# Folding two experts' partial sums in memory, and a queue of split work for VectorE and ScalarE

## The chip, the cores and the metric

The kernel runs on one core of a Trainium2 chip. The metric is device time in microseconds (us) of one execution; less is better. All matrix products run on TensorE (PE) with fp32 data. A product in enough precision takes three passes: each operand is split into a high part (`hi`, rounded to fp32r) and the rest (`lo = x - hi`), and hi·hi, lo·hi and hi·lo are added up in PSUM. ScalarE (ACT) writes the high parts, VectorE (DVE) the rests. GpSimd (POOL) and SyncE (SP) mostly issue DMAs.

## The reference

A gated linear recurrence over 768 steps (per batch and head) makes `x`, and a dense mixture of four experts is applied to it. Only the second part is touched here:

```python
# N, D, E, F = 3072, 384, 4, 1024
p = domain_probs / (domain_probs.sum(-1, keepdims=True) + 1e-09)
out = np.zeros((N, D), dtype=np.float32)
for e in range(E):
    h = np.maximum(x @ w1[e], 0.0)
    out += p[:, e:e + 1] * (h @ w2[e])
```

## The kernel before

**First phase** (to about 597 us). Twelve groups of 256 tokens. While DVE, ACT and DMAs make the recurrence of the next group, PE also applies experts 0 and 1 to the group before (`moe1`). At the end of each expert, `done` scales the two PSUM tiles by the token's probability on ACT and stores them with a DMA from POOL's queue into DRAM: `acc_d[g][e]`, one DRAM tile for each expert.

**Second phase** (597 us to the end). Experts 2 and 3, each over four blocks of 768 tokens, which makes eight rounds `R` = 0 to 7 (0 to 3 are expert 2). A block is two halves of 384 tokens (`u` = 0, 1). In a round there are four calls of `unit`, `j` = 0 to 3, each for two of the eight columns of hidden features. `unit` is a fast scheme of matrix multiplication: 11 products in place of 12, each 3 matmuls of 128x384, made from sums and differences of the weights (`prep_w`) and of the inputs (`prep_x`). It uses four PSUM banks `a`, `b`, `c`, `d` and these steps, in which a PSUM bank is added onto again after DVE has read what stood there:

- `a` and `m1` (ACT copies `a`), `b`, then `mp = b + m1` on DVE; `c`; `fill(0)`
- `b` goes on (product `s3`), so it needs `mp` to have been read; then `mq = b + m1`, `mq += c`, `d`, `mq += d` on DVE, ACT makes the hidden high part `hhb` of `mq`, DVE the rest `hlb`
- `a` goes on and gives another `hhb`, `hlb`; `fill(1)`
- `b` goes on (product `a22`), so it needs the first `mq` to have been read; then `m1 = b + m1` and its `hhb`, `hlb`
- `c` goes on; `mp = c + mp` and its `hhb`, `hlb`; `fill(2)`, `fill(3)`

The banks are taken in turn, so the next unit's `c` writes where this unit's `c` stood, and needs its `mp`. `fill(k)` puts in 9 matmuls of the second layer (`pob`) of an earlier hidden column. Round 0 has two fills in a unit, the later rounds four. Beside the `hlb` work, DVE adds each half's second layer into the accumulated output (`acc`, three instructions for each half, at `fill(1)` of the even units from round 1 on).

Between these steps `bg(k)` places work for later rounds, four places in a unit:

- `acc_add` (round 0 to 3, units 1 and 3): the two DRAM tiles of experts 0 and 1 were loaded by `acc_load` into `acc` and `prv`, and three DVE additions of 128x384 fold them.
- `prep_x` of the next round: 3 sums at the end of unit 2, and in unit 3 the splits of nine 128x384 inputs (`xh` on ACT, `xl` on DVE) with one more difference.
- `prep_w` of expert 3, four weight pairs, each begun in rounds 1, 2, 3 and 4: splits of weights (`whi`, `wlo`, `shi`, `slo`) and four short sums, spread one part at a time over the places 0 and 3 of units 0 to 2.

All DVE, ACT, SP and PE instructions of this phase are held to the order in which the code writes them (`pin`, `pe`), each engine runs its own list in order, and engines wait for one another by semaphores. The loads of inputs, weights and accumulated outputs are all in SP's list.

Of the kernel before, what the change touches and what calls it, by code (L numbers as in the profile page):

```python
# [16 lines left out]
HD = H * D  # L17
# [50 lines left out]
def fast_path(ctx, tc, qkP, aP, vP, probsP, w, out, flag):  # L68
# [34 lines left out]
    acc_d = [[dram.tile([P, CG, HD], F32, name=f"acc_d{g}_{e}") for e in range(E1)] for g in range(NG)]  # L103
# [125 lines left out]
    with ExitStack() as c1:  # L229
# [417 lines left out]
        def moe1(g, xh, xl, between=None, prev=None):  # L647
            def done(e, po):
                acc = moe.tile([P, CG, HD], F32, tag="acc", name=f"acc{g}_{e}")
                for t in range(CG):  # L650
                    nc.scalar.activation(acc[:, t, :], po[t], AF.Copy, scale=pr[:, g * CG + t, e:e + 1])
                nc.gpsimd.dma_start(acc_d[g][e], acc)
            mo.block(g, xh, xl, 0, NF1, done, between, prev)
# [172 lines left out]
    with ExitStack() as c2:  # L826
# [38 lines left out]
        def prep_w(e, j):  # L865
            i = e * FE + 2 * j
            sts = []
            for u in range(2):
                st = stage2(i + u)
                pin(nc.sync.dma_start(st, w[i + u]))  # L870
                sts.append(st)
            yield 0
            (st0, st1), hs = sts, []
            for u in range(2):
                hi2 = wpool.tile([P, 2 * HD], F32R, tag="whi", name=f"whi{i + u}")
                lo2 = wpool.tile([P, 2 * HD], F32R, tag="wlo", name=f"wlo{i + u}")
                split(hi2[:, u * P:], lo2[:, u * P:], sts[u][:, u * P:])
                hs.append((hi2, lo2))
                yield 2
            (h0, l0), (h1, l1) = hs  # L880
            if j % 2 == 0:
                shared[e] = (wpool.tile([P, 2 * HD], F32R, tag="whi", name=f"shi{i}"),
                             wpool.tile([P, 2 * HD], F32R, tag="wlo", name=f"slo{i}"))
            hs, ls = (x[:, (j % 2) * HD:(j % 2 + 1) * HD] for x in shared[e])
            s = stage2(i)[:, :4 * P]
            tt(s[:, cut(0)], st1[:, cut(0)], st1[:, cut(1)], ALU.add)
            tt(s[:, cut(1)], s[:, cut(0)], st0[:, cut(0)], ALU.subtract)
            tt(s[:, cut(2)], st0[:, cut(0)], st1[:, cut(0)], ALU.subtract)
            tt(s[:, cut(3)], st0[:, cut(1)], s[:, cut(1)], ALU.subtract)
            yield 2  # L890
            split(hs, ls, s[:, :3 * P])
            split(h1[:, cut(0)], l1[:, cut(0)], s[:, cut(3)])
# [8 lines left out]
            yield 2  # L901
# [17 lines left out]
        def prep_x(R, xs, X):  # L919
            (b11, b21, b31), (b12, b22, b32) = ([x[:, k, :] for k in range(NJ)] for x in xs)  # L920

            def put(nm, src):
                X[nm] = split(fin.tile([P, TB2], F32R, tag="xoh", name=f"xh{R}_{nm}", bufs=9),
                              fin.tile([P, TB2], F32R, tag="xol", name=f"xl{R}_{nm}", bufs=9), src)

            t2, t3 = (fin.tile([P, TB2], F32, tag=nm, name=f"{nm}_{R}", bufs=1) for nm in ("t2", "t3"))
            tt(t3, b22, b12, ALU.subtract)
            tt(b12, b12, b11, ALU.subtract)
            tt(t2, b22, b12, ALU.subtract)
            yield  # L930
            put("b11", b11)
            put("t2", t2)
            put("t1", b12)
            yield
            put("t3", t3)
            put("b21", b21)
            tt(b21, b21, t2, ALU.subtract)
            yield
            put("t4", b21)
            put("b32", b32)  # L940
            put("b31", b31)
            put("b22", b22)
            yield
# [26 lines left out]
        def unit(R, j, X, fill, bg):  # L970
# [12 lines left out]
            bg(0)  # L983
# [31 lines left out]
        def acc_load(R, u):  # L1015
            e, b = E1 + R // NB2, 2 * (R % NB2) + u
            got = []
            for t in range(C2):
                c = b * C2 + t
                acc = fin.tile([P, HD], F32, tag="acc2", name=f"acc2_{R}_{u}_{t}", bufs=6)  # L1020
                prv = None
                if e == E1:
                    pin(nc.sync.dma_start(acc, acc_d[c // CG][0][:, c % CG, :]))
                    prv = moe.tile([P, HD], F32, tag=("hh", "hl")[t % 2], name=f"prv{R}_{u}_{t}")
                    pin(nc.sync.dma_start(prv, acc_d[c // CG][1][:, c % CG, :]))
                else:
                    pin(nc.sync.dma_start(acc, acc2_d[c]))
                got.append((acc, prv))
            accs[R, u] = got
# [8 lines left out]
        def l2(R, u, f):  # L1038
# [13 lines left out]
            for t in range(C2):  # L1052
                c, acc = b * C2 + t, accs[R, u][t][0]
# [9 lines left out]
        for _ in prep_w(E1, 0):  # L1063
            pass
        for _ in prep_x(0, xs, X):
            pass
        for j in range(1, NP):
            for _ in prep_w(E1, j):
                pass
        held["on"] = True  # L1070
        jobs, new, nxt = [], {}, None
        late = {(1, 0): 0, (2, 0): 1, (NB2 - 1, 3): 2, (NB2, 0): 3}
        for R in range(NR2):
            for j in range(NP):
                if (R, j) in late:
                    jobs.append(prep_w(E1 + 1, late[R, j]))
                    next(jobs[-1])
                if j == 0:
                    acc_load(R, 0)
                    if R + 1 < NR2:  # L1080
                        nxt = prep_x(R + 1, load_x2(R + 1), new)
                if j == 2:
                    acc_load(R, 1)
# [8 lines left out]
                def bg(k, R=R, j=j):  # L1092
# [8 lines left out]
                unit(R, j, X, fill, bg)  # L1101
            if R + 1 < NR2:
                X = dict(new)
# [194 lines left out]
```

## Time and profile before

| What | us |
|---|---|
| median of 3 runs | 1005.82 (1005.23 to 1006.34) |
| the profiled execution | 1006.48 |
| its span in the profile | 1004.8 |
| busy: PE / weight loads / DVE / ACT / POOL | 966.6 / 939.5 / 744.7 / 409.9 / 48.4 |

The profile is of one execution. An engine's rows are groups or single instructions with their start, length and the idle time in front of them, with the engine and instruction that ended it. Buffer numbers are left out of names: `phb_3b` is bank `b` of unit 3 in any round. PE's instructions overlap: one of 128x384 is shown with about 0.33 us, but the next one starts 0.17 us after it.

### The profile page before, as it was taken

The numbers are of one execution on the slowest core, as the hardware profiler recorded it, in microseconds if no ns is written. First come the engines' busy times: TensorE is split into PE (matmuls) and PEld (weight loads), VectorE is DVE, ScalarE is ACT, GpSimd is POOL, SyncE is SP. The second block draws the span as 40 slices with busy tenths as digits, with TensorE's granted clock in tenths as the row PEclk, the third lists the DMA queues.
The fourth block names the chain that finished last, engine by engine and source line by source line (L and its number), as shares of the span: only waits on it lengthen the run. The fifth ranks groups of instructions, "written<-read, shape, count | busy, mean of one in ns | idle before, by whom it ended". The sixth has DMA issues, their size and how long they took to land.

```text
span 1004.8 us, 17383 instructions
## 1 busy us (share of the span) xinstructions
PE 966.6 (96%) x6810; PEld 939.5 (94%) x6810; DVE 744.7 (74%) x1610; ACT 409.9 (41%) x792; POOL 48.4 (5%) x90
## 2 busy tenths in 40 slices
PE   5899999999999999999999999899999899999997
PEld 2899998999999999999999999899999899999997
DVE  7789989798987989798942567867676777666651
ACT  7755525456364453636422443323222333222310
POOL 6030000000000000000000000000000000000000
PEclk9899999999999999999999999999999999999999
DMA  9585277474674836547171444132313242221111
GB/s 314 159 172 142 64 190 148 129 205 111 166 189 116 224 107 162 155 122 207 56 173 29 130 141 142 55 127 91 127 63 119 90 131 67 79 91 52 48 49 50
DMA packets 105131, 125.38 MB, mean 125 GB/s; under 512 B 7312, under 2 KB 91328, under 8 KB 105040
## 3 DMA queue, kind: packets, MB, share of 16 engines
q1 hardware_dynamic: 98928, 103.55, 37.5%
q0 software_dynamic: 6112, 20.63, 6.6%
q8 instruction: 55, 0.90, 0.4%
q14 instruction: 36, 0.29, 0.1%
HBM read 83.53 MB, written 40.62 MB: 124 GB/s over the span
## 4 chain that ended last, share of the span: by engine, by line


## 5 line engine op out<-in xcount | busy, mean ns | idle before, releaser
L198 PE MATMUL po<-whi,hh 128*128 128x384 f32 x384 | 129.6, 338 | 1.1 <-ACT hh L188 1.1
L198 PE MATMUL po<-wlo,hh 128*128 128x384 f32 x384 | 128.9, 336 | 0.0
L844 PE MATMUL pob<-whi,hlb 128*128 128x384 f32 x384 | 128.3, 334 | 0.0
L844 PE MATMUL pob<-whi,hhb 128*128 128x384 f32 x384 | 128.3, 334 | 0.0
L844 PE MATMUL pob<-wlo,hhb 128*128 128x384 f32 x384 | 128.3, 334 | 0.0
L198 PE MATMUL po<-whi,hl 128*128 128x384 f32 x384 | 124.1, 338 | 0.9 <-DVE hl L189 0.8
L188 ACT ACTIVATE hh<-ph 128x512 fp32r<-128x512 f32 x96 | 57.1, 595 | 145.0 <-PE ph L178 142.4
L178 PE MATMUL ph<-xha,whi 128*128 128x256 f32 x576 | 103.9, 286 | 1.2 <-ACT xha L165 1.2
L178 PE MATMUL ph<-xla,whi 128*128 128x256 f32 x576 | 100.9, 284 | 0.4 <-DVE xla L167 0.4
L178 PE MATMUL ph<-xha,wlo 128*128 128x256 f32 x576 | 101.3, 283 | 0.0
L189 DVE SCALAR_TENSOR_TENSOR hl<-ph,hh 128x512 fp32r<-128x512 f32 x96 | 66.0, 688 | 43.9 <-ACT hh L188 43.3
L178 PEld LDWEIGHTS ph<-xha,whi 128*128 128x128 f32 x576 | 85.9, 190 | 2.5 <-ACT xha L165 1.5
L178 PEld LDWEIGHTS ph<-xla,whi 128*128 128x128 f32 x576 | 82.5, 191 | 0.6 <-DVE xla L167 0.6
L178 PEld LDWEIGHTS ph<-xha,wlo 128*128 128x128 f32 x576 | 82.8, 190 | 0.2 <-issue 0.2
L198 PEld LDWEIGHTS po<-whi,hh 128*128 128x128 f32 x384 | 72.4, 189 | 1.5 <-ACT hh L188 1.3
L847 ACT ACTIVATE hhb<-mq 128x384 fp32r<-128x384 f32 x32 | 16.8, 526 | 138.9 <-DVE mq L850 138.9
L198 PEld LDWEIGHTS po<-whi,hl 128*128 128x128 f32 x384 | 70.9, 188 | 2.0 <-DVE hl L189 1.9
L198 PEld LDWEIGHTS po<-wlo,hh 128*128 128x128 f32 x384 | 72.5, 189 | 0.0
L844 PEld LDWEIGHTS pob<-whi,hlb 128*128 128x128 f32 x384 | 72.1, 188 | 0.0
L844 PEld LDWEIGHTS pob<-wlo,hhb 128*128 128x128 f32 x384 | 72.1, 188 | 0.0
L844 PEld LDWEIGHTS pob<-whi,hhb 128*128 128x128 f32 x384 | 72.1, 188 | 0.0
L532 PE MATMUL sc<-Qst,Kst 112*128 112x128 f32 x384 | 49.9, 280 | 1.1 <-ACT Kst L510 0.9
(380 smaller groups left out, 2040.2 us busy)
## 6 DMA issues: line engine op xcount, KB each, us to landing
qk<-qkP SPq DMA_DIRECT2D x24, 384.0 KB, 7.1
acc_d<-acc POOLq DMA_DIRECT2D x24, 384.0 KB, 3.3
acc<-acc_d SPq DMA_DIRECT2D x48, 192.0 KB, 2.9
A<-aP SPq DMA_DIRECT2D x22, 384.0 KB, 8.0
w2st<-w SPq DMA_DIRECT2D x16, 384.0 KB, 3.9
xb<-y_d SPq DMA_DIRECT2D x16, 384.0 KB, 5.0
q_d<-Q SPq DMA_DIRECT2D x12, 387.0 KB, 4.1
Qst<-q_d SPq DMA_DIRECT2D x12, 387.0 KB, 5.6
```

The costliest lines, as they stand in the source:

```text
L178: ins = nc.tensor.matmul(ph[:, u, :], wt[:, j * P:(j + 1) * P], xt[:, j, :], start=(n == 0), stop=(n == 3 * NJ - 1))
L188: wts["hh"] = nc.scalar.activation(hh, ph, AF.Relu)
L189: nc.vector.scalar_tensor_tensor(hl, ph, 0.0, hh, op0=ALU.max, op1=ALU.subtract)
L198: nc.tensor.matmul(po[t], ht[:, u, t * P:(t + 1) * P], wt[:, HD:], start=(i % FE == 0 and n == 0), stop=(i % FE == FE - 1 and n == 2))
L532: ins = nc.tensor.matmul(s_ps[:, h, :], Kc[:, hf * 4 + h, :], Qc[:, hf * 4 + h, :], start=True, stop=True)
L844: return tc.keep_in_program_order(nc.tensor.matmul(*args, **kw))
L847: pin(nc.scalar.activation(dst, src, fn))
```

## The change

Three things are changed.

1. Experts 0 and 1 share one DRAM tile for each group. Expert 0 stores into it, expert 1's DMA adds onto it (`accum_op=ALU.add`, from POOL's queue as before). `acc_load` then loads one tile in place of two, `acc_add` with its 24 additions is gone, and the loads of a half move from the start of units 0 and 2 to the start of units 1 and 3.
2. Splits and sums are items of one queue `side`. `bg(n)` takes `n` items; for a split it writes the ACT half, then the ACT half of the item behind it, and then the DVE half. The six places `at(0)` to `at(5)` of a unit take up to 4, 1, 2, 1, 1 and 4 items; place 2 of the even units takes none from round 1 on. A weight pair's five items (the four short sums as one of them, first) are put in at one unit start: pairs of rounds 1 and 2 at unit 1, the last two at units 0 and 1 of round 4.
3. In `unit`, `lo_h(R, 0, f1)` stands behind `mp = c + mp` and its `hi_h`.

```diff
-    acc_d = [[dram.tile([P, CG, HD], F32, name=f"acc_d{g}_{e}") for e in range(E1)] for g in range(NG)]
+    acc_d = [dram.tile([P, CG, HD], F32, name=f"acc_d{g}") for g in range(NG)]
...
-                nc.gpsimd.dma_start(acc_d[g][e], acc)
+                if e == 0:
+                    nc.gpsimd.dma_start(acc_d[g], acc)
+                else:
+                    nc.gpsimd.dma_start(acc_d[g], acc, accum_op=ALU.add)
...
         def split(hi, lo, src):
-            act(hi, src)
-            tt(lo, src, hi, ALU.subtract)
-            return hi, lo
+            return "split", (lambda: act(hi, src)), (lambda: tt(lo, src, hi, ALU.subtract))
+
+        side = []
+
+        def bg(n):
+            while n > 0 and side:
+                kind, first, second = side.pop(0)
+                if kind == "split":
+                    first()
+                if kind != "sum" and side and side[0][0] == "split":
+                    side[0][1]()
+                    side[0] = ("rest",) + side[0][1:]
+                second()
+                n -= 1
...
+            return [("sum", None, sums), split(h0, l0, st0), split(h1[:, P:], l1[:, P:], st1[:, P:]),
+                    split(hs, ls, s[:, :3 * P]), split(h1[:, cut(0)], l1[:, cut(0)], s[:, cut(3)])]
...
+            yield [put("b11", b11), put("t2", t2), put("t1", b12)]
+            yield [put("t3", t3)]
+            yield [put("b21", b21), ("sum", None, lambda: tt(b21, b21, t2, ALU.subtract))]
+            yield [put("b32", b32), put("t4", b21), put("b31", b31), put("b22", b22)]
...
             hi_h(R, 0, f0, a)
+            at(1)
             lo_h(R, 1, f1)
             lo_h(R, 0, f0)
             fill(1)
-            bg(1)
+            at(2)
             prod(b, W["a22"], X["t4"])
             prod(b, W["a23"], X["b31"], stop=True)
             tt(m1, b, m1, ALU.add)
             hi_h(R, 0, f1, m1)
+            at(3)
             prod(c, W["s4"], X["b22"])
             prod(c, W["a13"], X["b32"], stop=True)
-            lo_h(R, 0, f1)
             tt(p, c, p, ALU.add)
             hi_h(R, 1, f0, p)
-            bg(2)
+            lo_h(R, 0, f1)
+            at(4)
             lo_h(R, 1, f0)
             fill(2)
-            bg(3)
+            at(5)
             fill(3)
...
-        def acc_add(R, u):
-            for acc, prv in accs[R, u]:
-                if prv is not None:
-                    tt(acc, acc, prv, ALU.add)
...
+        room = (4, 1, 2, 1, 1, 4)
+        xat = {(2, 5): 0, (3, 0): 1, (3, 1): 2, (3, 2): 3, (3, 4): 4}
...
-                    if j in (1, 3) and k == 0:
-                        acc_add(R, j // 2)
-                    if R + 1 < NR2 and (j, k) in ((2, 3), (3, 0), (3, 1), (3, 3)):
-                        next(nxt)
-                    if jobs and j < 3 and (R == NB2 or k in (0, 3)):
-                        if next(jobs[0], None) is None:
-                            jobs.pop(0)
+                def at(k, R=R, j=j):
+                    if R + 1 < NR2 and (j, k) in xat:
+                        side.extend(next(parts))
+                    if not (R > 0 and j % 2 == 0 and k == 2):
+                        bg(room[k])
```

PE's list in the second phase is the same, instruction for instruction. What the engines now do in another order is seen best in two places of DVE's list. The first is the second half of unit 3 in round 0, with the inputs of round 1 being split (`m1_0_3` is `m1` of round 0, unit 3; `xl1_t3` the rest of input `t3` for round 1). Before:

```order
L850 TENSOR_TENSOR mq_0_3_7248<-phb0_3d_7288,mq_0_3_7248 128x384
L853 SCALAR_TENSOR_TENSOR hlb0_1_7_7303<-mq_0_3_7248,hhb0_1_7_7293 128x384
L853 SCALAR_TENSOR_TENSOR hlb0_0_6_7305<-phb0_3a_7242,hhb0_0_6_7301 128x384
L850 TENSOR_TENSOR xl1_t3_7308<-t3_1_7238,xh1_t3_7307 128x384
L850 TENSOR_TENSOR xl1_b21_7312<-xb1_0_6972,xh1_b21_7311 128x384
L850 TENSOR_TENSOR xb1_0_6972<-xb1_0_6972,t2_1_7237 128x384
L850 TENSOR_TENSOR m1_0_3_7246<-phb0_3b_7250,m1_0_3_7246 128x384
L853 SCALAR_TENSOR_TENSOR hlb0_0_7_7331<-m1_0_3_7246,hhb0_0_7_7323 128x384
L850 TENSOR_TENSOR mp_0_3_7247<-phb0_3c_7255,mp_0_3_7247 128x384
L853 SCALAR_TENSOR_TENSOR hlb0_1_6_7336<-mp_0_3_7247,hhb0_1_6_7334 128x384
L850 TENSOR_TENSOR xl1_t4_7348<-xb1_0_6972,xh1_t4_7347 128x384
L850 TENSOR_TENSOR xl1_b32_7352<-xb1_1_6975,xh1_b32_7351 128x384
```

And now, in the same place of the same engine:

```order
L853 TENSOR_TENSOR mq_0_3_7221<-phb0_3d_7258,mq_0_3_7221 128x384
L853 TENSOR_TENSOR xl1_t3_7274<-t3_1_7205,xh1_t3_7273 128x384
L856 SCALAR_TENSOR_TENSOR hlb0_1_7_7277<-mq_0_3_7221,hhb0_1_7_7263 128x384
L856 SCALAR_TENSOR_TENSOR hlb0_0_6_7279<-phb0_3a_7215,hhb0_0_6_7271 128x384
L853 TENSOR_TENSOR xl1_b21_7282<-xb1_0_6948,xh1_b21_7281 128x384
L853 TENSOR_TENSOR xb1_0_6948<-xb1_0_6948,t2_1_7204 128x384
L853 TENSOR_TENSOR m1_0_3_7219<-phb0_3b_7223,m1_0_3_7219 128x384
L853 TENSOR_TENSOR mp_0_3_7220<-phb0_3c_7228,mp_0_3_7220 128x384
L856 SCALAR_TENSOR_TENSOR hlb0_0_7_7304<-m1_0_3_7219,hhb0_0_7_7293 128x384
L853 TENSOR_TENSOR xl1_b32_7307<-xb1_1_6951,xh1_b32_7306 128x384
L856 SCALAR_TENSOR_TENSOR hlb0_1_6_7317<-mp_0_3_7220,hhb0_1_6_7302 128x384
L853 TENSOR_TENSOR xl1_t4_7309<-xb1_0_6948,xh1_t4_7308 128x384
```

`xl1_t3` moved ahead of two `hlb`, `mp` ahead of the `hlb` of `m1`, and `xl1_b32` in between the last two `hlb`. ACT's list there is unchanged but for `xh1_b32`, which now stands ahead of `xh1_t4`: its `xh1_t3` still stands behind the `hhb` of `mq` and of bank `a`, and its `xh1_b32` behind the `hhb` of `m1` and `mp`.

The second place is DVE in unit 1 of round 1, where the first weight pair of expert 3 is prepared (`w2st13` and `w2st14` are the loaded weights, `w2st15` the sums). Before:

```order
L850 TENSOR_TENSOR mp_1_1_7506<-phb1_1b_7509,m1_1_1_7505 128x384
L850 TENSOR_TENSOR acc2_1_0_0_7367<-acc2_1_0_0_7367,prv1_0_0_7369 128x384
L850 TENSOR_TENSOR acc2_1_0_1_7371<-acc2_1_0_1_7371,prv1_0_1_7373 128x384
L850 TENSOR_TENSOR acc2_1_0_2_7375<-acc2_1_0_2_7375,prv1_0_2_7377 128x384
L850 TENSOR_TENSOR w2st15_7532<-w2st14_7365 128x128
L850 TENSOR_TENSOR w2st15_7532<-w2st15_7532,w2st13_7363 128x128
L850 TENSOR_TENSOR w2st15_7532<-w2st13_7363,w2st14_7365 128x128
L850 TENSOR_TENSOR w2st15_7532<-w2st13_7363,w2st15_7532 128x128
L850 TENSOR_TENSOR mq_1_1_7507<-phb1_1b_7509,m1_1_1_7505 128x384
```

And now:

```order
L853 TENSOR_TENSOR mp_1_1_7469<-phb1_1b_7472,m1_1_1_7468 128x384
L853 TENSOR_TENSOR w2st15_7337<-w2st14_7335 128x128
L853 TENSOR_TENSOR w2st15_7337<-w2st15_7337,w2st13_7333 128x128
L853 TENSOR_TENSOR w2st15_7337<-w2st13_7333,w2st14_7335 128x128
L853 TENSOR_TENSOR w2st15_7337<-w2st13_7333,w2st15_7337 128x128
L853 TENSOR_TENSOR wlo24_7341<-w2st13_7333,whi24_7340 128x768
L853 TENSOR_TENSOR wlo25_7343<-w2st14_7335,whi25_7342 128x640
L853 TENSOR_TENSOR slo24_7339<-w2st15_7337,shi24_7338 128x384
L853 TENSOR_TENSOR mq_1_1_7470<-phb1_1b_7472,m1_1_1_7468 128x384
```

The three additions are gone, and the three long weight rests, which stood in three other places of units 0 and 1 (one of them, `slo24`, behind the last `hlb` of unit 1), now stand together between `mp` and `mq`. In round 4 the pairs of units 0 and 1 stand in the same way.

More of the change, by code (lines that the diff above doesn't have):

```diff
@@ L871, in prep_w @@
                 sts.append(st)
[L872 to L880, printed above, removed]
+            st0, st1 = sts
+            s = stage2(i)[:, :4 * P]
             if j % 2 == 0:
[L882 to L883 removed]
+                shared[e] = [wpool.tile([P, 2 * HD], F32R, tag=f"w{nm}", name=f"s{nm}{i}") for nm in ("hi", "lo")]
+            (h0, l0), (h1, l1) = ([wpool.tile([P, 2 * HD], F32R, tag=f"w{nm}", name=f"w{nm}{i + u}")
+                                   for nm in ("hi", "lo")] for u in range(2))
             hs, ls = (x[:, (j % 2) * HD:(j % 2 + 1) * HD] for x in shared[e])
[L885 to L892, printed above, removed]
             def both(hi, lo, n):
@@ L1075, in fast_path @@
                 if (R, j) in late:
[L1076 to L1083, printed above, removed]
+                    jobs.append(((R, j + 1) if R < NB2 - 1 else (NB2, late[R, j] - 2), prep_w(E1 + 1, late[R, j])))
+                if jobs and jobs[0][0] == (R, j):
+                    side += jobs.pop(0)[1]
+                if j == 0 and R + 1 < NR2:
+                    parts = prep_x(R + 1, load_x2(R + 1), new)
+                if j % 2 == 1:
+                    acc_load(R, j // 2)
                 def fill(k, R=R, j=j):
```

68 lines of the change are left out of this document (24 added, 44 removed).

## The prediction

> **What bounds the kernel now.** I read the busy time of each engine by stretches first, then the waits of PE in the second phase, then those of DVE, and then single rows of the stretches in which PE waits. Columns of the first: the stretch and its length, busy time (and instructions) of PE, PEld, DVE, ACT and POOL, granted clock, DMA share, GB/s.
>
> ```profile
> 600.00:800.00 200.00, 188.28 (x1061) 183.07 (x1060) 141.73 (x279) 60.97 (x130) 10.41 (x20) 1.00 0.32 102
> 800.00:975.00 175.00, 175.00 (x1011) 175.00 (x1010) 112.69 (x222) 49.65 (x106) 2.96 (x6) 1.00 0.24 77
> ...
> 100.00:575.00 475.00, 471.17 (x3810) 458.13 (x3807) 381.15 (x844) 217.81 (x404) 10.80 (x20) 1.00 0.54 141
> ```
>
> PE is the bound, at full clock. From 800 us on it is never idle: 175 / 1011 = 0.173 us for a matmul. From 600 to 800 us, which is expert 2, it is idle for 200 - 188.3 = 11.7 us, and does 1061 matmuls where 200 / 0.173 = 1155 would fit. The 94 missing are 16.3 us; by adding up the excess over 0.173 between the starts of all its rows there I get 16.0 (a wait costs another 0.1 to 0.3 us, since the matmuls behind it start slowly). So 16.0 us is all that this change can gain in the second phase. Who is late (waiter, what for, us in total, times, longest), and what DVE itself does and waits for there:
>
> ```profile
> PE phb_0b L844 <- DVE mp L850: 4.3, 4, 1.1
> PE phb_3b L844 <- DVE mq L850: 3.5, 4, 2.2
> PE phb_0c L844 <- DVE mp L850: 1.6, 1, 1.6
> PE phb_1b L844 <- DVE mq L850: 0.9, 1, 0.9
> ...
> DVE hlb L853 <- ACT hhb L847: 29.3, 49, 0.7
> DVE acc L850 <- DMA prv<-acc_d: 13.3, 13, 1.8
> ...
> L850 DVE TENSOR_TENSOR acc<-acc,prv 128x384 f32<-128x384 f32 x24 | 13.0, 555 | 13.3 <-DMA prv<-acc_d 13.3
> ```
>
> All of PE's waits are for DVE, always for an `mp` or `mq` that stands in DVE's list behind other work. It isn't DVE's total (142 of 200 us): it is late in unit 3 and just behind it, where input splits and `acc_add` come together.
>
> **The additions.** 24 of them with 13.0 us of busy time (1.4 for a half, since they start 0.47 apart) and 13.3 us of waiting for `prv` leave DVE's list. Their cover now is nothing: in unit 3 they stand right ahead of the `mq` for which PE waits. Rows of round 0's unit 3 and of the start of round 1 (PE, DVE, ACT):
>
> ```profile
> 624.05 0.33 PE L844 MATMUL phb_3a<-xh_b,whi 128*128 128x384 f32 x1
> 627.89 0.44 PE L844 MATMUL phb_3b<-xh_t,shi 128*128 128x384 f32 x1 [0.56 <-DVE mp L850]
> 631.17 0.44 PE L844 MATMUL phb_3b<-xh_t,whi 128*128 128x384 f32 x1 [0.90 <-DVE mq L850]
> 637.74 0.41 PE L844 MATMUL phb_0c<-xh_t,shi 128*128 128x384 f32 x1 [1.60 <-DVE mp L850]
> 641.14 0.45 PE L844 MATMUL phb_0b<-xh_t,shi 128*128 128x384 f32 x1 [1.08 <-DVE mp L850]
> ...
> 627.29 0.55 DVE L850 TENSOR_TENSOR mp<-phb_3b,m 128x384 f32<-128x384 f32 x1
> 627.75 1.49 DVE L850 TENSOR_TENSOR acc<-acc,prv 128x384 f32<-128x384 f32 x3
> 630.56 0.55 DVE L850 TENSOR_TENSOR mq<-phb_3b,m 128x384 f32<-128x384 f32 x1
> 631.81 0.56 DVE L850 TENSOR_TENSOR mq<-phb_3d,mq 128x384 f32<-128x384 f32 x1
> 632.96 0.56 DVE L853 SCALAR_TENSOR_TENSOR hlb<-mq,hhb 128x384 fp32r<-128x384 f32 x1 [0.59 <-ACT hhb L847]
> 635.43 0.55 DVE L850 TENSOR_TENSOR m<-phb_3b,m 128x384 f32<-128x384 f32 x1
> 637.04 0.55 DVE L850 TENSOR_TENSOR mp<-phb_3c,mp 128x384 f32<-128x384 f32 x1
> 640.53 0.55 DVE L850 TENSOR_TENSOR mp<-phb_0b,m 128x384 f32<-128x384 f32 x1
> ...
> 632.40 0.53 ACT L847 ACTIVATE hhb<-mq 128x384 fp32r<-128x384 f32 x1 [4.00 <-DVE mq L850]
> 632.83 0.47 ACT L847 ACTIVATE hhb<-phb_3a 128x384 fp32r<-128x384 f32 x1
> 633.20 0.51 ACT L847 ACTIVATE xh_t<-t 128x384 fp32r<-128x384 f32 x1
> ```
>
> **The order within a unit.** Before, `m1`, wait 0.59, `hlb`, `mp`, wait 0.59, `hlb` takes 3.24 us to the next instruction. With `mp` ahead of the first `hlb`, ACT works beside DVE: starts 0.47 apart and a wait of some 0.2 make 2.1, so 1.1 us less in each unit. Where DVE waits for PE anyway it is worth nothing.
>
> Now I work through DVE's new list for that unit, from its first matmul at 624.05 as zero. PE without waits needs `mp` read at 18 matmuls (3.12), `mq` at 30 (5.19), next unit's `c` at 51 + 6 (9.87), and next unit's `mp` at 51 + 18 (11.94). DVE: the last `mp` stood at 3.24, now 1.1 sooner, 2.1, done at 2.65: the wait of 0.56 goes. Three splits (0.47 each) and `mq` at 3.97, done at 4.5: the wait of 0.90 goes. The third `mq` ends at 5.78. ACT then does `hhb`, `hhb`, `xh_t` (0.03 behind DVE, starts 0.43 and 0.37 apart): `xh_t` is done at 7.13. `xl1_t3` stands next on DVE, so DVE now waits 1.4 us where it waited 0.59. It goes on at 7.16: `xl1_t3`, two `hlb`, `xl1_b21`, a difference (0.58), `m1` at 9.63, `mp` at 10.1, done at 10.65. PE wants `c` at 9.87: a wait of 0.9. Then `hlb` at 10.76; `xl1_b32` has to wait for ACT, which does `hhb`, `hhb`, `xh_b` first, to 11.66; four more at 0.47 bring the next `mp` to 14.0, done at 14.55. PE, moved by 0.9, wants it at about 12.9: a wait of 1.7. With slow starts that leaves 2.7 us at this one boundary, nearly what stands there now (1.60 + 1.08 and starts).
>
> **The other boundaries** have a longer unit 3 (four fills, 69 matmuls, 11.94 us). The undisturbed pattern is the boundary of rounds 5 and 6, with the old order and no additions:
>
> ```profile
> 875.38 0.33 PE L844 MATMUL phb_3a<-xh_b,whi 128*128 128x384 f32 x1
> 890.46 0.33 PE L844 MATMUL phb_0b<-xh_t,shi 128*128 128x384 f32 x1
> ...
> 884.10 0.55 DVE L850 TENSOR_TENSOR m<-phb_3b,m 128x384 f32<-128x384 f32 x1
> 889.21 0.55 DVE L850 TENSOR_TENSOR mp<-phb_0b,m 128x384 f32<-128x384 f32 x1
> ...
> 900.61 0.56 DVE L850 TENSOR_TENSOR mp<-phb_1b,m 128x384 f32<-128x384 f32 x1 [1.07 <-ACT m L847]
> ```
>
> There `mp` is done 0.70 us before PE wants it (889.76 against 890.46). In the new order `m1` comes 0.8 later (the wait for `xh_t`) and from `m1` to that `mp` 4.4 us pass in place of 5.1, so `mp` is done some 0.1 later: 0.6 us to spare, no wait. Without the additions all boundaries behind round 1 look like this one, so I take their waits (8.3 of the 16.0 us, summed over the rows behind 680 us) as gone.
>
> **The weight items** stand together ahead of `mq` now: four sums, `wlo`, `wlo`, `slo`.
>
> ```profile
> 656.42 0.28 DVE L850 TENSOR_TENSOR w2st<-w2st 128x128 f32<-128x128 f32 x1
> 656.74 0.69 DVE L850 TENSOR_TENSOR w2st<-w2st,w2st 128x128 f32<-128x128 f32 x3
> 641.00 0.95 DVE L850 TENSOR_TENSOR wlo<-w2st,whi 128x768 fp32r<-128x768 f32 x1
> 650.41 0.82 DVE L850 TENSOR_TENSOR wlo<-w2st,whi 128x640 fp32r<-128x640 f32 x1
> 714.23 0.55 DVE L850 TENSOR_TENSOR slo<-w2st,shi 128x384 fp32r<-128x384 f32 x1
> ```
>
> That is 0.93 + 0.95 + 0.82 + 0.55 = 3.3 us between `mp` and `mq`, which from round 1 on has until matmul 39, 6.75. In units 1, `mp` starts 1.31 behind the unit (900.61; the unit begins at 899.30, two units behind 875.38): `mq` at 5.0, done at 5.6, 1.2 us to spare. In round 4's unit 0, behind the input splits, `mp` starts at 2.0: `mq` is done at 6.3, 0.5 to spare. ACT has its halves done by then. So no wait, and the one of 0.9 for `phb_1b` goes. DVE's total falls, so nothing piles up into the next unit. At lower bound these items cost nothing; at upper bound the 0.5 is wrong and the two dense units of round 4 cost about 1 us each.
>
> **The DMAs.** SP issues 24 loads fewer. A half's load now comes three units ahead of its use. The accumulating store's price is not in the trace; the nearest rows are two loads of the same size on POOL's queue, plain (`whi`) and accumulating (`wlo`), and the plain store:
>
> ```profile
> POOL acc_d L652 <- ACT acc L651: 524.4, 24, 33.1
> ...
> acc_d<-acc POOLq DMA_DIRECT2D x24, 384.0 KB, 3.3
> ...
> whi<-w POOLq DMA_DIRECT2D x8, 384.0 KB, 5.7
> wlo<-w POOLq DMA_DIRECT2D x8, 384.0 KB, 7.0
> ```
>
> Accumulating lands 1.3 us later. Nobody in the first phase waits for it: POOL itself idles 524 us, its buffer comes back two experts later, and the load comes in the second phase. So I take 0; ends: -0 (the bytes no longer loaded as `prv` free no wait of PE beyond those counted) and, if all 12 held PE up by 1.3, 15.6. [...]
>
> **The sum.** 16.0, less 2.7 left at the first boundary, less 0.15 for a small wait of `phb_1a` at 605.2 us that is untouched: 13.1 us. Against the profiled execution, 1006.48 - 13.1 = 993.4; it stood 0.7 over the median, so 992.7 by that. I say 993.0.
>
> **Rivals.** A measurement of this kernel can tell about 0.2%, 2 us, from no change.
>
> - *DVE now lags behind ACT.* `xl1_t3` and `xl1_b32` stand where ACT has two `hhb` ahead of them. My 0.5 to 0.6 us to spare rest on hand-overs of 0.03 to 0.1. If the five in that chain cost 0.2 more each, DVE is 1.0 later at seven boundaries: 0.4 and a slow start of 0.3 at six, 2.0 at the first, 6 us in all, also in rounds 5 to 7, which had none. Time 999. For it: the slack is thin. Against: 0.59 repeats to 0.01 in the rows.
> - *Everything goes.* If ACT gets to `xh_t` sooner than I think, the first boundary loses its 2.7 too: 990.5.
> - *It doesn't do what it says.* ACT isn't ahead: its list differs by one swap beside the weights, and if the waits were PE's own they would stay: 1005 to 1006. Against: every wait of PE in that stretch names DVE.
> - *Slower: the accumulating stores hold up the first phase's transfers.* They share the DMA engines with the loads on which the recurrence hangs. If each costs PE 1.3 us, 15.6 less 13.1 makes 1008; it decides from 1.1 us each. [...]
>
> **Numbers.** Likeliest 0.72 (its own range 991.5 to 996), lag 0.14, everything 0.05, no effect 0.04, slower 0.05. Faster is 0.72 + 0.14 + 0.05 = 0.91. The range leaves out the upper half of the lag, the no-effect and the slower case, and the best end of the second: 990.5 to 998.5.
>
> **What the changed kernel's profile would show.** Right: from 650 to 975 us PE idles under 1 us, and `phb_0c` and `phb_0b` still wait some 0.9 and 1.7 us once, at the first boundary; DVE's wait for `prv` is gone, `xl_t` waits for ACT 1.4 us in each unit 3. Wrong: `phb_0b` waiting at every boundary (lag), `phb_0b` in round 4's unit 0 waiting for `mq` (weights too dense), or PE idle time in 100 to 575 us grown from 3.8 us (stores).

## The result, and the profile after

The changed kernel takes 995.6 us (median; 994.34 to 997.21), the kernel before beside it 1005.9. The ratio is 0.9899 (95% interval 0.9882 to 0.9916), so 10.3 us are gained. Forecast was 993.0, with a range of 990.5 to 998.5. The profiled execution took 995.35 us, with a span of 993.7.

Stretches as before the change (length; busy time and instructions of PE, PEld, DVE, ACT, POOL; clock, DMA share, GB/s):

```profile
600.00:800.00 200.00, 197.81 (x1138) 196.69 (x1138) 140.40 (x281) 66.39 (x142) 12.15 (x22) 1.00 0.27 86
100.00:575.00 475.00, 470.20 (x3787) 457.26 (x3787) 378.76 (x838) 215.86 (x401) 14.28 (x20) 1.00 0.56 141
```

From 600 to 800 us PE is idle for 2.2 us in place of 11.7, and from 650 to 975 us it is busy without a break. In the first phase it is idle for 4.8 in place of 3.8. All waits of PE in the second phase (the first two lines), and three of DVE's waits there:

```profile
PE phb_0b L847 <- DVE mp L853: 1.5, 1, 1.5
PE phb_0c L847 <- ACT hhb L850: 0.7, 1, 0.7
...
DVE hlb L856 <- ACT hhb L850: 15.3, 32, 0.6
...
DVE xl_t L853 <- ACT xh_t L850: 9.7, 7, 1.4
```

Six kinds of waits of PE became two, once each, both at the first boundary. (The one at `phb_0c` is put down to ACT's `hhb`, which ended 0.05 us ahead of the matmul. The matmul starts 0.146 us behind the end of DVE's `mp`. In the kernel before it starts 0.146 us behind `mp` too, where the `hhb` had ended 1.2 us earlier. So it waits for `mp` here too, as the prediction had it.) DVE's wait for `prv` is gone, its wait for `hhb` fell from 29.3 us to 15.3, and the new one of `xl_t` for ACT came seven times with 1.4 us, as forecast.

Now the two phases apart. The first `phb_0a` matmul begins the second phase, at 597.35 us before the change and at 599.30 after it. From there to the end of the span it is 407.45 us before and 394.40 after: **the second phase is 13.05 us shorter** (forecast 13.1), and **the first phase was 1.95 us longer** in this execution (forecast 0). Their difference, 11.1, is what separates the two profiled executions (1006.48 and 995.35). On chip C, below, the same kernel gained 11.2 us, and 13.2 us in a second set of runs. The first phase lost its time in one place: the gap between the stores that stood at 341.4 and 371.6 us before grew by 2.8 us. There the score matmuls, rows of before and of after, and the granted clock after, by stretches:

```profile
348.17 2.02 PE L532 MATMUL sc<-Qst,Kst 112*128 112x128 f32 x16
```

```profile
348.67 3.59 PE L532 MATMUL sc<-Qst,Kst 112*128 112x128 f32 x16 [1.20 <-issue]
```

```profile
346.00:349.00 3.00, 1.80 (x16) 1.71 (x16) 1.56 (x5) 0.00 (x0) 0.00 (x0) 0.92 1.05 315
349.00:352.00 3.00, 3.00 (x16) 3.00 (x16) 1.16 (x2) 0.00 (x0) 0.00 (x0) 0.51 0.78 307
```

PE waits 1.20 us for `Kst`: the row names no releaser, but this load lands at 348.58 us, 0.1 us ahead of the matmul. An adding store, issued 8 us before the matmul, is under way beside it (8.6 us to landing; 13.3% of the 16 DMA engines' time from 335 to 352 us), and for some 3 us behind the wait the clock is half (0.51). The wait and the 1.6 us by which the 16 matmuls are slower make 2.8. The experiments had two questions: what each part of the change gives in the second phase, and whether the adding store is to blame for the first.

### The profile page after: what moved, and what is told of

It reads as the page before. It is cut to its first block, busy times and chain, and to the rows that moved or that the text cites. A ratio compares the mean times of both kernels' runs of the same rounds, so it can differ in the third digit from the quotient of the medians.

```text
span 993.7 us, 17323 instructions
## 1 busy us (share of the span) xinstructions
PE 964.9 (97%) x6810; PEld 941.2 (95%) x6810; DVE 731.7 (74%) x1586; ACT 408.8 (41%) x792; POOL 52.8 (5%) x90
## 4 chain that ended last, share of the span: by engine, by line
```

## The experiments

They ran on three chips, called B, C and D, each time beside the kernel before; A is the first pair. Excess is the time that PE loses by waits in the second phase. It is added up from the first `phb_0a` on: wherever two starts are 0.23 us or more apart, what lies above 0.173 us. The kernel before has 16.1 us by this count (the prediction had 16.0) and the changed one 2.9. The last column, median less excess, is the time that the second phase's waits don't explain; the excess in it is that of the one profiled execution.

| Chip, kernel | Expert 1's store | Second phase begins, us | its length, us | excess, us | median, us | ratio to before (95%) | median - excess |
|---|---|---|---|---|---|---|---|
| A before | plain | 597.35 | 407.5 | 16.1 | 1005.9 | | 989.8 |
| A changed | adding | 599.30 | 394.4 | 2.9 | 995.6 | 0.9899 (0.9882 to 0.9916) | 992.7 |
| B before | plain | | | (15.8) | 1003.5 | | 987.7 |
| B plain store | plain | 595.28 | 394.0 | 2.9 | 991.0 | 0.9880 (0.9864 to 0.9895) | 988.1 |
| B merging alone | adding | 595.08 | 396.3 | 5.0 | 993.8 | 0.9899 (0.9883 to 0.9914) | 988.8 |
| B late splits | adding | 596.79 | 392.9 | 1.6 | 991.1 | 0.9867 (0.9851 to 0.9883) | 989.5 |
| C before | plain | | | (15.8) | 1004.6 | | 988.8 |
| C order alone | plain | 596.32 | 413.4 | 22.1 | 1011.6 | 1.0066 (1.0046 to 1.0085) | 989.4 |
| C changed, again | adding | 595.63 | 394.4 | 2.9 | 993.4 | 0.9891 (0.9874 to 0.9908) | 990.5 |
| C changed, third | adding | 594.78 | 394.0 | 2.9 | 991.4 | 0.9867 (0.9852 to 0.9883) | 988.5 |
| C carried splits | adding | 595.19 | 392.4 | 1.3 | 989.3 | 0.9847 (0.9833 to 0.9860) | 988.0 |
| D before, again | plain | 595.79 | 406.7 | 15.5 | 1004.6 | 0.9996 (0.9985 to 1.0007) | 989.1 |
| D carried once | adding | 594.89 | 391.9 | 0.5 | 990.0 | 0.9847 (0.9834 to 0.9860) | 989.5 |
| D `hlb` first | adding | 595.43 | 403.8 | 12.6 | 1000.9 | 0.9955 (0.9942 to 0.9968) | 988.3 |
| D nearly all adding | adding | 598.72 | 394.5 | 2.9 | 997.0 | 0.9917 (0.9902 to 0.9932) | 994.1 |

In brackets: no profile on that chip, the mean of the two others.

**Merging alone**: the DRAM tile and the adding store put into the kernel before, its order kept.

```diff
...
-                    pin(nc.sync.dma_start(acc, acc_d[c // CG][0][:, c % CG, :]))
-                    prv = moe.tile([P, HD], F32, tag=("hh", "hl")[t % 2], name=f"prv{R}_{u}_{t}")
-                    pin(nc.sync.dma_start(prv, acc_d[c // CG][1][:, c % CG, :]))
+                    pin(nc.sync.dma_start(acc, acc_d[c // CG][:, c % CG, :]))
```

> The kernel before, with one DRAM tile for both experts, the adding store, and no prv loads and additions; order and places of all other work are those of before. Theory, the additions and their waits were most of PE's 16.0 us: the boundary of rounds 0 and 1 keeps waits of about 0.7, 1.5 and 1.3 us (3.8 us with slow restarts), one of 0.9 us stays between units 0 and 1 of round 0, the later boundaries have none, so PE's excess in the second phase is about 5 us and the time about 994.8 us, or 996.8 us if the first phase loses the 2 us that it lost in the changed kernel's profile. Rival, the order of the splits does half of the gain: excess of 8 us or more, time of 998 us or more.

PE's waits in the second phase:

```profile
PE phb_0c L847 <- DVE mp L853: 1.4, 1, 1.4
PE phb_0b L847 <- DVE mp L853: 1.1, 1, 1.1
PE phb_1c L847 <- DVE mp L853: 0.8, 1, 0.8
PE phb_3b L847 <- DVE mp L853: 0.6, 1, 0.6
```

The excess is 5.0 us, as expected, and nothing is left behind the first boundary. Measured from the 15.8 us that the kernel before has in the mean of its two profiles, merging alone takes 10.8 of the 12.9 us.

Merging removes two things at once, the additions and DVE's waits for the `prv` loads, and no run parts them. The kernel before shows that from round 1 on the waits can be the larger part. Two of the three additions ahead of the longest wait of PE (2.16 us):

```profile
780.20 0.56 DVE L850 TENSOR_TENSOR acc<-acc,prv 128x384 f32<-128x384 f32 x1 [1.41 <-DMA prv<-acc_d]
782.19 0.56 DVE L850 TENSOR_TENSOR acc<-acc,prv 128x384 f32<-128x384 f32 x1 [1.44 <-DMA prv<-acc_d]
```

Whether earlier loads with two DRAM tiles would have won most of the 10.8 us wasn't tried.

**The order alone**: the queue and the swap, with two DRAM tiles, `prv` loads and additions. It was run on chip B (ratio 1.0057, 1.0040 to 1.0075) and on chip C, whose profile is used below.

```diff
...
+                if j == 0:
+                    acc_load(R, 0)
...
+                if j == 2:
+                    acc_load(R, 1)
...
+                    if j in (1, 3) and k == 0:
+                        acc_add(R, j // 2)
```

> The changed kernel's queue and order of splits, but with two DRAM tiles, plain stores, prv loads at the start of units 0 and 2 and the three additions at the first place of units 1 and 3, ahead of the queue's items. Theory, with the additions in DVE's list the order is worth nothing: PE's excess in the second phase stays near 16 us, since the weight items now follow right behind the additions (units 1 of rounds 1 and 2 wait 2 to 3 us for mq, unit 3 of each round of expert 2 about 2 us); time 1003 to 1006 us. Rival, the order gains by itself about a third of the 13 us: excess of 11 us, time about 1001 us.

> The queue and order alone, with two DRAM tiles, prv loads and additions, run for a second profile, since the first was taken at a granted clock of 0.85. Its time stood 6 us over the kernel before where 0 to 3 under it were expected. Theory, the whole of that is in the second phase, where additions and weight items now stand in one row ahead of mq: PE's excess there is about 22 us against 16.0. Rival, the second phase has 16 us as expected, and the 6 us lie in the first phase, which begins the second one 6 us later.

The three largest of PE's waits in the second phase, then one of them with what follows it, and the clock there:

```profile
PE phb_1b L844 <- DVE mq L850: 6.0, 3, 2.5
PE phb_0b L844 <- DVE mp L850: 5.7, 4, 1.5
PE phb_3b L844 <- DVE mq L850: 2.0, 3, 1.2
```

```profile
656.31 0.58 PE L844 MATMUL phb_1b<-xh_t,whi 128*128 128x384 f32 x1 [2.46 <-DVE mq L850]
656.69 0.53 PE L844 MATMUL phb_1b<-xh_t,wlo 128*128 128x384 f32 x1
657.01 0.53 PE L844 MATMUL phb_1b<-xl_t,whi 128*128 128x384 f32 x1
```

```profile
656.00:660.00 4.00, 3.69 (x12) 3.69 (x13) 3.07 (x7) 1.27 (x3) 0.00 (x0) 0.57 0.01 4
```

The order alone makes the kernel slower by 7 us; the second phase has an excess of 22.1, and its start is no later than elsewhere. My first expectation had the waits for `mq` in units 1 (2 to 3 us, where the weight items now follow the additions) but put those in units 3 too high (about 2 us each; 0.2 to 1.2 came). It didn't have the three waits of 1.4 us for `mp` at the later boundaries, nor what stands behind the two waits of 2.5 us: eleven and ten matmuls start 0.32 us apart, not 0.17.

**`hlb` first**: the changed kernel with its third part undone.

```diff
+            lo_h(R, 0, f1)
             tt(p, c, p, ALU.add)
             hi_h(R, 1, f0, p)
-            lo_h(R, 0, f1)
```

> The changed kernel with part 3 undone: the hlb of m1 stands ahead of mp again. Theory, the swap saves DVE 1.06 us in each unit, and where DVE is late PE pays it: the waits of 0.7 us of phb_1c and 0.6 us of phb_3b in round 0 are back, the wait at phb_0c at the first boundary grows from 0.7 to about 1.8 us, and six later boundaries, which had 0.6 us to spare, wait 0.1 to 0.5 us each at phb_0b; PE's excess in the second phase is about 6.5 us (5.7 to 9) against 2.85, the time 3 to 6 us over the changed kernel. Rival, the swap is hidden, since DVE waits for PE or ACT behind it: excess within 0.5 us of 2.85.

PE's longest waits in the second phase:

```profile
PE phb_0b L847 <- DVE mp L853: 2.9, 7, 0.6
PE phb_0c L847 <- DVE mp L853: 1.9, 1, 1.9
PE phb_1c L847 <- DVE mp L853: 0.8, 1, 0.8
PE phb_3b L847 <- DVE mp L853: 0.5, 1, 0.5
```

The waits are where they were expected: 1.9 us at `phb_0c` (1.8), and six later boundaries with 0.39 each; one of 0.3 for `acc` came beside them. The excess is 12.6 and not 6.5. A wait shown as 0.39 is a loss of 0.66 from start to start, 4.0 us for the six: the wait is counted from the shown end of the matmul ahead, 0.16 us behind the place where the next one could start, and the matmul behind it starts 0.1 late. The wait for `acc` is a loss of 0.6. And the boundary of rounds 0 and 1 ran at half clock for 6.7 us. What this slowed ahead of 639.00 falls into the wait for `mp`; the matmuls behind it cost some 2 us:

```profile
639.00 0.69 PE L847 MATMUL phb_0b<-xh_t,shi 128*128 128x384 f32 x1 [0.58 <-DVE mp L853]
```

```profile
636.30:643.00 6.70, 6.12 (x19) 5.61 (x19) 4.55 (x10) 1.84 (x5) 0.00 (x0) 0.50 0.55 168
```

So with the queue in place the swap of two lines is worth 9.7 us in this profile, some 2 of them by the clock. The parts don't add up: merging alone gives 10.8, order and swap alone lose 6.3, merging and queue without the swap give 3.2, all three 12.9. The queue pays only once the additions and the 1.06 us in each unit are out of DVE's list.

**The plain store**, to see if the adding store delays the first phase:

```diff
-                    nc.gpsimd.dma_start(acc_d[g], acc, accum_op=ALU.add)
+                    nc.gpsimd.dma_start(acc_d[g], acc)
```

> The changed kernel, with expert 1's partial sums stored over those of expert 0 instead of added to them (it leaves out the addition of expert 0's part). Theory A, the adding store takes longer (median landing 4.9 us over both kinds of stores, 3.3 before) and so delays the loads on which the first phase hangs: the stores land in about 3.3 us again, the wait of 1.2 us of a score matmul (sc) near 348 us is gone, PE idles about 3.8 us between 100 and 575 us, the first phb_0a matmul stands near 597.3 us as before the change (599.3 after it), and the time is about 993.4 us, 2 us under the changed kernel. Theory B, the first phase differs from run to run whatever the store is: the phb_0a matmul stands anywhere from 597.3 to 599.5 us, and the time has the same median as the changed kernel, 995 to 996 us. In both, PE's excess in the second phase is the changed kernel's 2.9 us.

The score matmul waited 0.4 us, also with a plain store. The second phase began at 595.28, earlier than either theory had it, but with the adding store of "merging alone" on the same chip it began at 595.08. Median less excess is 988.1 us here, against 988.8 and 989.5 for the two kernels with adding stores. So the plain store doesn't take the wait away, and what it may save, 0.7 to 1.4 us, is within the spread of the runs.

**The changed kernel again**, and a version with the store held back:

> The changed kernel once more, unaltered, beside the kernel before on one chip. Theory A, the adding stores cost first-phase time: the wait of the score matmul near 348 us is there again with 1.0 us or more, and the phb_0a matmul that begins the second phase stands 1 us or more behind the 595.1 to 595.3 us seen in the best profiles so far. Theory B, the first phase varies by itself: the wait may be anything from 0 to 1.2 us. In both, PE's excess in the second phase is 2.8 to 3.0 us, since nothing there depends on the first phase. Time: the kernel before less 10 to 12 us.

Near 348 us there was no wait (one of 0.2 us stood at 304 us), and the second phase began at 595.63. The excess of the second phase repeats to 0.1 us, the first phase only to some microseconds. Over all runs, a wait of 1 us or more near 348 us came in two of the eight profiles with twelve adding stores (1.20 us in the first one, 1.05 in "late splits") and in none of the four with plain ones. The awaited `Kst` load took 6.1 to 7.7 us beside adding stores and 6.2 to 6.9 beside plain ones. These are too few to tell the two apart.

```diff
+                    if kept:
+                        nc.gpsimd.dma_start(*kept.pop(), accum_op=ALU.add)
...
+                    kept.append((acc_d[g], acc))
```

> The changed kernel, with each adding store of a group held back until the plain store of the next group's first expert, 16 to 33 us later, so that it no longer falls on the load of Kst in the group near 340 us. Theory A, the adding store takes twice the engine time of a plain one (13.3% against 6.7% of the 16 DMA engines in the same 17 us) and the awaited Kst load behind it lands later: the score matmul near 348 us waits under 0.3 us, and the second phase begins 0.8 us or more sooner than in the unaltered changed kernel of the same chip. Theory B, the store has no part in it: the wait is 0.4 us or more with no adding store in the 10 us ahead of it, and the median time is within 0.5 us of the changed kernel's.

This test failed: the first phase isn't held to the order of the code, and the scheduler put each adding store back to where its data were ready (the one in question at 339.92 us), so every engine's list is that of the changed kernel. It serves as its third profile, "changed, third" in the table: no wait near 348 us, and a median 2 us below the other run of the same lists on the same chip.

**The kernel before again**:

> The kernel before, unaltered, for a second profile on a chip other than the first one's. Theory A, the adding stores cost the changed kernel about 2 us in the first phase everywhere: here the first phb_0a matmul stands at 593 to 593.5 us, 2 us ahead of the 594.8 to 595.6 us of the changed kernel's later profiles. Theory B, they cost nothing that can be told from the scatter, and the first profile's 599.3 was one execution: phb_0a stands between 594.8 and 596.5 us. In both, PE's excess in the second phase is 15.7 to 16.0 us again, and the time 1003 to 1006 us.

It began its second phase at 595.79 us. With plain stores in expert 1's place four profiles stand at 595.28 to 597.35 (mean 596.2), with adding ones there and plain ones in expert 0's place eight at 594.78 to 599.30 (mean 595.9). So the late start of the first profile is no rule. By the last column of the table, adding less the kernel before is +2.9 on chip A, +1.1 and +1.8 on B, +1.7, -0.3 and -0.8 on C, +0.4 and -0.8 on D: 0.7 us in the mean, with a standard deviation of 1.4. The two altered kernels with plain stores stand at +0.4 (B) and +0.6 (C) by the same count. A cost of a microsecond or so can't be excluded, nor is one shown; 2 us in every run isn't what the runs have.

**Nearly all stores adding**:

```diff
-                if e == 0:
-                    nc.gpsimd.dma_start(acc_d[g], acc)
+                k = g - g % 6
+                if e == 0 and g == k:
+                    nc.gpsimd.dma_start(acc_d[k], acc)
...
-                    nc.gpsimd.dma_start(acc_d[g], acc, accum_op=ALU.add)
+                    nc.gpsimd.dma_start(acc_d[k], acc, accum_op=ALU.add)
...
```

> The changed kernel with 22 of the 24 stores of the first phase adding in place of 12: groups 0 to 5 and 6 to 11 are all added onto one DRAM tile each (the second phase reads these sums, so the output is another). Everything else stands as it was. Theory A, each adding store costs the first phase 0.1 to 0.2 us: ten more of them begin the second phase 1 to 2 us later than the 594.8 to 596.8 us of the other profiles of these chips, and the median is 994.5 us or more. Theory B, the transfer takes twice the engine time of a plain one but nobody waits for it: the second phase begins within 594.8 to 596.8 us, and the median stays within 991 to 994 us. In both, landings of acc_d have a median near 6 us, and the excess in the second phase is 2.85 us.

PE's waits for the score loads in the first phase:

```profile
PE sc L532 <- issue: 1.1, 2, 0.9
...
PE sc L532 <- DMA Kst<-k_d: 0.9, 1, 0.9
```

The second phase begins 3.3 to 3.8 us later than in the two other changed kernels of chip D, and median less excess is 994.1 against 988.3 and 989.5. This is theory A's side, and more than it had, for stores in expert 0's place: ten of them cost 4 to 6 us. That they share a DRAM tile isn't the reason: in the profile each is issued 0.3 to 0.6 us behind its data, as before, so none waits for the store ahead of it. (The median of all landings, expected near 6 us, was 4.9.) An adding store isn't free, then. That the twelve of the changed kernel cost less because mostly nobody waits for the loads beside them is argued from PE's waits, not shown by a run.

**What is left at the first boundary**: two versions of the changed kernel that move input splits. Late: `t3` goes behind the two `hlb`, the last four splits behind the last `hlb`. Carried: besides, three of those four go behind the next unit's first `mp`; once: only from round 0 to 1. The edit of the last:

```diff
-        xat = {(2, 5): 0, (3, 0): 1, (3, 1): 2, (3, 2): 3, (3, 4): 4}
+        xat = {(2, 5): (0,), (3, 0): (1,), (3, 2): (2, 3), (3, 5): (4,)}
...
-                        bg(room[k])
+                        bg(3 if (j, k) == (3, 2) else 1 if (R, j, k) == (0, 3, 5) else room[k])
```

> The changed kernel, with the input split t3 behind the two hlb of unit 3's middle (DVE no longer waits 1.4 us there for ACT's xh_t) and the last four input splits behind the last hlb of unit 3. Theory, what is left of PE's excess is the first boundary, and there DVE's waits for ACT set it: the wait of PE for hhb at phb_0c (0.7 us) goes, that for mp at phb_0b becomes about 1.3 us, so the excess falls from 2.9 to about 1.7 us and the time by 1.2 us against the changed kernel. DVE's xl_t waits for ACT fall from 9.7 us in 7 to under 2 us. Rival, the boundary is set by DVE's total of work: the wait moves over to phb_0b, excess and time stay within 0.3 us.

> The changed kernel with the input splits of unit 3 spread further: t3 behind the two hlb, and of the last four items (b32, t4, b31, b22) one at the end of unit 3 and three carried into the first place of the next unit 0, behind its first mp. Theory, DVE's list just ahead of that mp is all that the first boundary hangs on: mp is done some 12.0 to 12.3 us behind the unit's start where PE wants it at 11.9, so PE's excess in the second phase falls from 2.9 to 0.3 to 0.6 us, and the time by 2.4 us against the changed kernel. Rival, the carried splits make unit 0 late: phb_0b waits for mq in round 4's unit 0 (weight items and three input splits together) or a product of unit 0 waits for xl_b22, 0.5 us or more at several boundaries, and nothing is gained.

> The kernel with carried input splits, but carried only over the boundary of rounds 0 and 1; behind every other round all four last splits stand at the end of unit 3, as in the kernel with late splits. Theory, the new wait of 0.6 us of a pob matmul for acc in round 4 came from three carried splits that stand beside the weight items there, and no other boundary needs the carrying: that wait goes and none comes back, PE's excess in the second phase is 0.3 to 0.6 us (1.2 with all boundaries carried, 2.85 in the changed kernel), the time 2.4 us under the changed kernel. Rival, the wait for acc comes from ACT or from the weight items alone: it stays with 0.4 us or more, and the excess with 1.1 us or more.

PE's only wait with late splits, and with all boundaries carried:

```profile
PE phb_0b L847 <- DVE mp L853: 1.1, 1, 1.1
```

```profile
PE pob L847 <- DVE acc L856: 0.6, 1, 0.6
```

Late splits: 1.6 us of excess (1.7 expected). Carried: 1.3 in place of 0.3 to 0.6, through a new wait in round 4. There the carried splits take the first place of the unit, and `wlo`, moved behind `mq`, waits for its ACT half ahead of `hlb`, `hlb` and `acc` in DVE's list:

```profile
781.20 0.96 DVE L853 TENSOR_TENSOR wlo<-w2st,whi 128x768 fp32r<-128x768 f32 x1 [1.70 <-ACT whi L850]
782.08 0.55 DVE L856 SCALAR_TENSOR_TENSOR hlb<-mq,hhb 128x384 fp32r<-128x384 f32 x1
782.54 0.55 DVE L856 SCALAR_TENSOR_TENSOR hlb<-phb_0a,hhb 128x384 fp32r<-128x384 f32 x1
783.01 1.66 DVE L856 SCALAR_TENSOR_TENSOR acc<-pob,pr,acc 128x384 f32<-128x384 f32 x3
```

Carried once: 0.5 us, no wait above 0.15 us left in the second phase. At 0.9847 of the kernel before (0.9834 to 0.9860) this version is faster than that, and by the second phase's excess 2.4 us better than the changed kernel. By the median it isn't told apart from the best runs of the changed kernel (0.9867, 0.9852 to 0.9883) or from the other carried version.

## Why the prediction was right, and where not

**The sum of the second phase** was 13.1 us; 13.05 came, and 13.2 by the excess (16.1 less 2.9). That it agrees to 0.05 is partly chance: up to the start of the last matmul 13.4 us are gained, and the stretch behind that one, 6.7 us long and not 6.3, gives 0.3 back. It was right for the reason given, since each step of the worked boundary stands in the trace. Rows of DVE and PE there after the change:

```profile
627.04 0.55 DVE L853 TENSOR_TENSOR mp<-phb_3b,m 128x384 f32<-128x384 f32 x1
628.91 0.55 DVE L853 TENSOR_TENSOR mq<-phb_3b,m 128x384 f32<-128x384 f32 x1
632.10 0.56 DVE L853 TENSOR_TENSOR xl_t<-t,xh_t 128x384 fp32r<-128x384 f32 x1 [1.38 <-ACT xh_t L850]
634.57 0.55 DVE L853 TENSOR_TENSOR m<-phb_3b,m 128x384 f32<-128x384 f32 x1
635.04 0.55 DVE L853 TENSOR_TENSOR mp<-phb_3c,mp 128x384 f32<-128x384 f32 x1
636.59 0.56 DVE L853 TENSOR_TENSOR xl_b<-xb,xh_b 128x384 fp32r<-128x384 f32 x1 [0.32 <-ACT xh_b L850]
638.94 0.55 DVE L853 TENSOR_TENSOR mp<-phb_0b,m 128x384 f32<-128x384 f32 x1
...
624.95 0.33 PE L847 MATMUL phb_3a<-xh_b,whi 128*128 128x384 f32 x1
635.73 0.41 PE L847 MATMUL phb_0c<-xh_t,shi 128*128 128x384 f32 x1 [0.70 <-ACT hhb L850]
639.54 0.44 PE L847 MATMUL phb_0b<-xh_t,shi 128*128 128x384 f32 x1 [1.49 <-DVE mp L853]
```

With the unit's first matmul at 624.95 as zero, `mp` starts at 2.09 (2.1), `mq` at 3.96 (3.97), `xl_t` at 7.15 (7.16), `m1` at 9.62 (9.63), `mp` at 10.09 (10.1), `xl_b` at 11.64 (11.66) and the next `mp` at 13.99 (14.0); in brackets what was worked out. The two waits are shown as 0.70 and 1.49 where 0.9 and 1.7 were forecast; counted between starts, as the forecast was, they are 0.86 and 1.66, and with the slow starts 2.7 us, as worked out.

- *The additions*: confirmed by "merging alone", 10.8 us, together with the waits for `prv`; in "order alone", where they stay, the loss is back with interest.
- *The order within a unit*, 1.1 us: confirmed by undoing it. "Where DVE waits for PE anyway it is worth nothing" held for the unit, but I used the swap only at boundaries and didn't see how much hung on it. The 0.6 to spare at the later ones, less the 1.06 that the swap saves, is -0.46, and the measured wait there is 0.39.
- *The other boundaries*: 0.6 us to spare. At round 5 to 6 `mp` is done at 878.35 and PE reads at 879.01, 0.66:

```profile
877.80 0.55 DVE L853 TENSOR_TENSOR mp<-phb_0b,m 128x384 f32<-128x384 f32 x1
...
879.01 0.33 PE L847 MATMUL phb_0b<-xh_t,shi 128*128 128x384 f32 x1
```

- *The weight items*: no wait, as forecast. `mq` is done 1.4 us ahead of PE in units 1 and 0.8 in round 4's unit 0 (1.2 and 0.5 were worked out). What more work beside them costs is seen from "order alone" (additions ahead of them: 2.5 us) and "carried" (three splits more: 0.6).
- *The accumulating store*, taken as 0. This is the step whose argument has a fault. The sign that I had named (idle time of PE in the first phase grown from 3.8 us) came, 4.8, but it doesn't repeat: the seven other profiles with the same twelve stores have 3.2 to 4.4 us, the four with plain stores 3.7 to 4.0. The 2.6 us by which the median stands over the forecast are of the size of the first profile's 1.95. The term that I bounded by `wlo` against `whi`, 1.3 us of landing, is larger for the stores themselves. A store with nothing beside it (524 to 536 us: packets, MB, share of 16 engines, and landing), before and after:

```profile
q0 software_dynamic: 80, 0.39, 8.2%
acc_d<-acc POOLq DMA_DIRECT2D x1, 384.0 KB, 2.6
```

```profile
q0 software_dynamic: 144, 0.39, 24.4%
acc_d<-acc POOLq DMA_DIRECT2D x1, 384.0 KB, 4.8
```

Landing takes 2.2 us longer, 1.8 times as long (4.8 / 2.6), where `wlo` against `whi`, on which I leaned, has 1.2 (7.0 / 5.7). The DMA engines are held 3.0 times as long for the same bytes (24.4 / 8.2). Among other loads near 340 us it is about twice (13.3 against 6.9 in the same 17 us). "Nobody in the first phase waits for it" is true of the store itself; it overlooked the loads beside it. Four loads issued 0.5 to 2.8 us behind another store (251 to 262 us), before and after:

```profile
k_d<-K SPq DMA_DIRECT2D x4, 192.0 KB, 3.8
```

```profile
k_d<-K SPq DMA_DIRECT2D x4, 192.0 KB, 4.8
```

The last two of the four land 3.8 to 4.0 us behind their issue in every profile with plain stores (3.8 and 3.9 before the change), and 4.9 to 5.5 us in every one with adding stores (5.0 and 5.1 after it). Here PE doesn't wait for them; where it does, the delay can count. What that cost in the changed kernel stays open: 2 us in the first profile, 0.7 in the mean, not told from zero. With ten more such stores in other places it was 4 to 6.

The rivals: no lag (all later boundaries clear), and not everything went, since ACT was where I put it; it took a move of the input splits to clear that boundary. "It doesn't do what it says" is out, since merging alone took 10.8 us of PE's waits. The slower rival's mechanism exists, at well under its deciding price of 1.1 us for each store: the ten stores in expert 0's place cost 0.4 to 0.6 us each.

## What to carry to other kernels

Write out the late engine's list for one unit, with starts from the rows, as far as the place where the other engine needs it: here each start came out within 0.02 us, and a few tenths to spare decided whether 1 us in a unit was worth nothing or 10 us. Changes to the order of a full list are not additive, so each is tested with the others in place. A store that nobody waited for took 22.5% of the DMA engines' time from 251 to 262 us here, in place of 9.7%, and four loads beside it landed in 4.8 us in place of 3.8; somebody may wait for such loads. Look at what is in flight beside a transfer before its price is set to zero.

## What the runs showed of the hardware

PE's clock went to half behind short waits. It did so for about 3 us behind waits of 2.46 us ("order alone", 0.57 in the 4 us shown) and of 1.20 us (the first profile after the change, 0.51), and for 6.7 us from 1.1 us behind a wait of 1.86 us ("`hlb` first", 0.50). It didn't behind the 1.05 us of "late splits" (1.00), nor behind 2.16 us in the kernel before, row and clock:

```profile
784.68 0.44 PE L844 MATMUL phb_3b<-xh_t,whi 128*128 128x384 f32 x1 [2.16 <-DVE mq L850]
```

```profile
784.40:788.00 3.60, 3.32 (x19) 3.33 (x20) 2.87 (x7) 1.73 (x4) 0.00 (x0) 1.00 0.00 0
```

So the length of a wait alone doesn't decide it, and such a stretch costs some 1.6 to 2 us beside the wait. What does decide it stays open.

And lists that are the same on every engine, run on one chip, had medians 2 us apart (993.4 and 991.4). In a kernel like this, a gain of that size is read from the waits and not from the time.
